# Clustered attention with experts on one core: one tile for the halves of q and k, and placing as ten single steps

## Chip, core and metric

The kernel runs on one NeuronCore of one Trainium2 chip. The metric is device microseconds of one execution; the kernel before took 1026.75 us in the median of 3 runs (1024.31 to 1026.94).

## What is computed

Two things in a row: attention within clusters, over 4 batches x 8 heads x 768 positions of 64 values, with 16 centroids per head, and on its output, as 3072 rows of 512, a layer of 8 experts of which each row uses two. Cut to what matters:

```python
q_n, k_n, c_n = (t / (norm(t) + 1e-6) for t in (q, k, centroids))
q_assign = argmax(einsum('bhsd,hcd->bhsc', q_n, c_n), -1)
k_assign = argmax(einsum('bhsd,hcd->bhsc', k_n, c_n), -1)
scores = where(q_assign[..., :, None] == k_assign[..., None, :], scale * q @ k.T, -1e9)
attn = exp(scores - max(scores))
attn = attn / (attn.sum(-1) + 1e-9)
x = (attn @ v), heads put side by side            # 3072 x 512
logits = x @ w_gate
noisy = logits + log1p(exp(x @ w_noise)) * noise
top2, weights = two largest of noisy, softmax of them
out[row] = sum over its two experts of weight * (relu(x @ w1[e]) @ w2[e])
```

## The kernel before

**Tiling.** Attention works on 16 pairs of heads (4 batches x 4 pairs). A pair takes 12 steps: 2 heads s, 6 chunks kc of 128 keys each. There are 192 steps t in one loop; the values of a step are multiplied 4 steps after its scores. The experts follow behind the loop, on the same engines; their code is not touched.

**One pair p**, in the order in which its work is due:

- `load_qk` (L581) brings q and k of both heads into a tile qt by a DMA on SP's queue; `load_v` (L592) brings v of two pairs.
- `a_hi` (L641) on ScalarE (ACT) and `a_lo` (L654) on VectorE (DVE) split float32 q and k into a high half and the rest, in pieces of 384 columns. They go into a tile **hl** of [128, 4, 768], whose four parts are k low, q high, k high and q low. From pair 2 on, ACT first copies a piece of qt into a PSUM bank (L651), writes the high half from there (L652), and DVE writes the low half (L660). Each pair allocates a new tile named hl from a pool with one buffer, so all lie in the same memory; pair 1 has another tile, xt.
- `b_place` (L722) is ten DMAs on SP's queue (the very first on ACT's) that copy parts of hl to the partitions where the score matmuls read them: into A (L427; three buffers, pair p uses p mod 3) and into Bt, called B in the profile. Four of them go from 64 partitions with 2 x 768 columns, two from 32 partitions with 2 x 768, and four from 32 partitions with 768.
- `a_sims` to `a_eq` find each position's cluster, `a_mask` (L708) turns the clusters into mask rows mk, and `b_mask` (L734) copies them into A with four DMAs.
- `b_max` (L741): PE multiplies halves and mask in A into a PSUM bank (m<-A, L748) and DVE takes the row maxima out of it (mm, L750); 24 of them per pair, in pieces of 128 queries x 384 keys. `b_neg` (L752) makes the negated maxima in high and low halves (nm, L758 to L761); `b_negT` (L763) has PE transpose them (L766) and ACT copy them to nt (L768), and a DMA puts nt into Bt.
- `scores` (L772): for each key chunk and each half of the queries PE multiplies A with A (e<-A, L779) and adds Bt with Bt (e<-B, L780), and ACT writes the exponentials (pe, L781) out of that bank. The two banks e0 and e1 take turns, so a score matmul waits until ACT has emptied its bank. `split_p` (L784) makes the low part pl of the exponentials on GpSimd (POOL; DVE for the last pairs), and `values` (L795) multiplies both parts with v.
- `x_hi` and `x_lo` split a pair's output x into halves xh, `x_put` (L888) stores them to DRAM (xs) on SP's queue, and `x_turn` (L895) copies them transposed into xt. `zero_out` (L852) writes zeros to the output on the same queue, a piece at a time.

**What sets the order.** Every helper call is given a time by `attention()`, and a table MOVE shifts it: the key is the helper's name and arguments (or 'all' for every pair past the first few), the value a number of slots, each a third of a step, and a rank within the slot. The text list FIRST holds the calls ahead of the loop. Each engine and each DMA queue does its work in the order in which the calls come. SP issues a DMA only after the ones ahead of it in its program are issued, and each issue may wait for semaphores. A DMA's end is counted on one of eight semaphores (DMAHW0 to DMAHW7), taken in turn.

In the loop a step's scores stand between the first and second third, and the values of the step four back between the second and the last:

```python
slot(0)
if 0 <= t < z:
    self.scores(t // 12, (t % 12) // 6, t % 6)
if 0 <= t - 1 < z:
    self.split_p((t - 1) // 12, ((t - 1) % 12) // 6, (t - 1) % 6)
slot(1)
...
slot(2)
```

Of the kernel before, what the change touches and what calls it, by code (L numbers as in the profile page):

```python
# [10 lines left out]
F32R = mybir.dt.float32r  # L11
# [86 lines left out]
    ('b_max', 'all', 1, 2, 0): (-1, -3),  # L98
    ('b_max', 'all', 1, 2, 1): (-1, 3),
    ('b_max', 'all', 1, 3, 0): (-1, 0),  # L100
    ('b_max', 'all', 1, 3, 1): (2, 3),
    ('b_max', 'all', 1, 4, 0): (-1, 0.5),
# [20 lines left out]
    ('b_max', 2, 0, 0, 1): (-3, 0),  # L123
# [1550 lines left out]
```

## Time and profile before

| | before |
|---|---|
| median of 3 runs | 1026.75 us (1024.31 to 1026.94) |
| the profiled execution, its own time | 1021.25 us |
| its span in the trace | 1019.4 us |
| PE busy | 943.3 us (93%), 7985 instructions |
| PE weight loads | 613.6 us (60%) |
| DVE busy | 653.6 us (64%) |
| ACT busy | 489.2 us (48%) |
| POOL busy | 568.2 us (56%) |
| mean granted clock of PE | 0.975 |

The span is what the trace shows from first to last instruction; the execution's own time holds 1.85 us more. Weight loads run beside matmuls. The granted clock is that of TensorE: 1.00 is 2.4 GHz, 0.50 is 1.2 GHz, and a figure between them is a mean over time at either. Attention's loop fills the span up to about 456 us, the experts the rest.

### The profile page before, as it was taken

What the parts mean: (1) busy time and instruction counts of PE and PEld (TensorE: products, weight loads), DVE (VectorE), ACT (ScalarE), POOL (GpSimd) and SP (SyncE); (2) the same over time, 40 slices, a digit from 0 to 9 for tenths busy, and PEclk for the clock granted to TensorE, in tenths of its full rate; (3) what the DMA queues carried; (4) which work ended last, traced back from release to release, by engine and by line L of the source; (5) the groups of instructions that cost most, each with busy time, mean ns of one, the idle gap of its engine ahead of it and who ended that gap; (6) DMA issues with size and microseconds to landing.
All of it is one profiled execution on the core that took longest, in us unless ns stands there. A gap on an engine that the chain in (4) does not pass through costs nothing. (4 is left out here: it accounts for less than half of the span.)

```text
span 1019.4 us, 21147 instructions
## 1 busy us (share of the span) xinstructions
PE 943.3 (93%) x7985; PEld 613.6 (60%) x7985; DVE 653.6 (64%) x1401; ACT 489.2 (48%) x1080; POOL 568.2 (56%) x640
## 2 busy tenths in 40 slices
PE   4779899998989899899889999999999999999994
PEld 2567788787868787774455545445455454554542
DVE  5768788797869788986636655546554655555420
ACT  2567677776777766477042415315233153241510
POOL 9558698887999899962435225234243252432311
PEclk9989999998989999999989999999999999999997
DMA  7687798988887776154395925929529267292200
GB/s 191 167 197 172 167 233 204 222 201 213 198 203 190 188 166 139 67 98 118 120 215 153 256 86 155 216 74 245 147 84 265 93 167 216 67 256 89 69 32 31
DMA packets 147148, 162.28 MB, mean 159 GB/s; under 512 B 85433, under 2 KB 112441, under 8 KB 147042
## 3 DMA queue, kind: packets, MB, share of 16 engines
q1 hardware_dynamic: 133612, 123.60, 49.3%
q0 software_dynamic: 12864, 36.37, 12.0%
q10 hardware_dynamic: 566, 0.91, 0.5%
q8 instruction: 64, 1.05, 0.5%
q14 instruction: 42, 0.34, 0.1%
HBM read 77.30 MB, written 26.05 MB: 101 GB/s over the span
## 5 line engine op out<-in xcount | busy, mean ns | idle before, releaser
L792 POOL TENSOR_TENSOR pl<-pe 128x768 f16<-128x768 f32 x173 | 251.3, 1468 | 47.3 <-ACT pe L781 38.1
L750 DVE TENSOR_REDUCE mm<-m 128x1 f32<-128x384 f32 x384 | 198.3, 550 | 47.9 <-PE m L748 47.2
L1561 PEld LDWEIGHTS <-w1t 128*128 128x128 f16 x1536 | 149.8, 98 | 118.3 <-DMA xT<-xg 7.8
L781 ACT ACTIVATE pe<-e 128x384 f32<-128x384 f32 x384 | 167.9, 488 | 94.5 <-PE e L780 87.7
L1602 PEld LDWEIGHTS <-hT 128*128 128x128 f16 x1152 | 112.2, 98 | 133.9 <-issue 1.1
L1614 POOL DMA_INDIRECT out<-yo,idx x50 | 60.2, 1204 | 229.9 <-DVE yo L1610 109.4
L1561 PE MATMUL m<-xT,w1t 128*128 128x400 f16 (+4 forms) x768 | 171.8, 335 | 0.0
L779 PE MATMUL e<-A 128*128 128x384 f32 x384 | 143.3, 373 | 16.3 <-ACT pe L781 16.1
L748 PE MATMUL m<-A 128*128 128x384 f32 x384 | 133.1, 396 | 13.6 <-DMA A<-mk 8.9
L780 PE MATMUL e<-B 128*128 128x384 f32 x384 | 133.7, 348 | 2.5 <-issue 2.5
L1602 PE MATMUL m<-w2t,hT 128*128 128x512 f16 x600 | 132.0, 379 | 0.0
L1561 PE MATMUL e<-xT,w1t 128*128 128x400 f16 (+4 forms) x528 | 122.1, 336 | 7.4 <-DMA xT<-xg 7.4
L1437 DVE TENSOR_TENSOR hT<-hr,hT 128x384 f16<-128x384 f32 (+6 forms) x128 | 70.7, 557 | 78.4 <-ACT hT L1436 77.4
L813 PE MATMUL av<-vv,pe 128*128 128x65 f16 x1152 | 100.4, 197 | 0.0
L815 PE MATMUL av<-vv,pe 128*128 128x64 f16 x1152 | 98.8, 195 | 0.0
L1541 POOL DMA_INDIRECT xg<-xs,idx x50 | 52.6, 1051 | 79.3 <-DMA xT<-xg 69.3
L748 PEld LDWEIGHTS m<-A 128*128 128x128 f32 x384 | 73.6, 200 | 35.5 <-DVE mm L750 13.5
L813 PEld LDWEIGHTS <-pe 128*128 128x128 bf16 x1152 | 78.2, 99 | 23.9 <-issue 20.5
L779 PEld LDWEIGHTS e<-A 128*128 128x128 f32 x384 | 75.6, 197 | 22.1 <-ACT pe L781 19.2
L1434 ACT ACTIVATE hr<-e 128x400 f32<-128x400 f32 (+4 forms) x44 | 22.3, 507 | 137.8 <-PE e L1561 137.8
L815 PEld LDWEIGHTS <-pe 128*128 128x128 bf16 x1152 | 80.4, 100 | 0.0
L1602 PE MATMUL e<-w2t,hT 128*128 128x512 f16 x360 | 79.8, 379 | 0.6 <-ACT w2t L1441 0.5
(282 smaller groups left out, 1448.0 us busy)
## 6 DMA issues: line engine op xcount, KB each, us to landing
stg<-in_moe_w SPq DMA_DIRECT2D x64, 512.0 KB, 4.0
qt<-in_qk SPq DMA_DIRECT2D x15, 768.0 KB, 10.4
A<-hl SPq DMA_DIRECT2D x30, 384.0 KB, 3.7
B<-hl SPq DMA_DIRECT2D x29, 384.0 KB, 6.9
vt<-in_v SPq DMA_DIRECT2D x8, 768.0 KB
out<-zt SPq DMA_DIRECT2D x12, 512.0 KB
A<-hl SPq DMA_DIRECT2D x60, 96.0 KB, 6.5
xs<-xh SPq DMA_DIRECT2D x15, 384.0 KB, 3.5
```

What stands on the lines that cost most here:

```text
L748: nc.tensor.matmul(t, A[:, s, 0, j * 128:j * 128 + 128], A[:, s, 1, n * 384:n * 384 + 384], start=True, stop=True)
L750: nc.vector.tensor_reduce(st["mm"][:, self.NJ * s + j, n:n + 1], t, axis=X, op=OP.max, negate=True)
L779: nc.tensor.matmul(t, A[:, s, 1, ks], A[:, s, 0, ns], start=True, stop=False)
L780: nc.tensor.matmul(t, Bt[:, 0, s, ks], Bt[:, 1, s, ns], start=False, stop=True)
L781: nc.scalar.activation(pe[:, n], t, AF.Exp, scale=self.scale)
L792: (nc.vector if last else nc.gpsimd).tensor_tensor(lo, pe, hi, op=OP.subtract)
L813: nc.tensor.matmul(av[:, j, :], ph[:, js], vv[:, hh, kj, 64:129], start=(kc == 0 and j == 0), stop=False, skip_group_check=True)
L815: nc.tensor.matmul(av[:, j, :64], ph[:, js], vv[:, hh, kj, 0:64], start=False, stop=False, skip_group_check=True)
L1437: nc.vector.tensor_tensor(h1, r[:, a:b], h0, op=OP.subtract)
L1561: nc.tensor.matmul(p, self.w1t[:, wi, c, f * 128:f * 128 + 128], self.xT[e][:, c, xi, n0:n1], start=(i == 0), stop=(i == 3 * ND - 1))
L1602: nc.tensor.matmul(p, self.hT[:, hi, f, t * 128:t * 128 + 128], self.w2t[:, wi, f], start=(i == 0), stop=(i == 3 * NF - 1))
L1614: i = nc.gpsimd.indirect_dma_start(out=self.out, out_offset=bass.IndirectOffsetOnAxis(ap=en[:r], axis=0), in_=yo[:r], in_offset=None, boun ...
```

## The change

- **One tile for the halves.** The tile hl is allocated once, for pair 0, and kept as `self.hl`; pair p from 2 on writes its halves into the same tile. Pair 1 keeps its xt.
- **Placing as ten single steps.** `b_place`, two calls per pair that issue six and four DMAs, becomes `p_hi`, `p_lo` and `p_b` (one DMA each per head s) and `p_a` (one for each head and each of q and k), each with its own time and its own entry in MOVE. The DMAs themselves, their sources, targets and sizes stay.
- **New places.** About 150 entries of MOVE are new, gone or changed, and FIRST has another order. No arithmetic changes.

```diff
 MOVE
...
-    ('a_eq', 2): (-2, 0),
+    ('a_eq', 1): (73, 0),
...
-    ('a_hi', 'all', 0, 0): (1, 3),
-    ('a_hi', 'all', 0, 1): (2, -3),
+    ('a_hi', 'all', 0, 0): (2, 3),
+    ('a_hi', 'all', 0, 1): (1, -3),
...
-    ('a_lo', 'all', 0, 0): (1, -0.5),
-    ('a_lo', 'all', 0, 1): (3, 0.5),
+    ('a_lo', 'all', 0, 0): (2, -0.5),
+    ('a_lo', 'all', 0, 1): (2, 0.5),
...
-    ('a_mask', 2): (-3, 0),
+    ('a_mask', 2): (-1, 0),
...
+    ('b_max', 'all', 0, 0, 0): (4, 0),
+    ('b_max', 'all', 0, 0, 1): (2, 0),
...
-    ('b_place', 'all', 0): (0, 0.5),
-    ('b_place', 'all', 1): (6, 0.5),
...
+    ('load_v', 'all', 1): (-3, 0),
+    ('p_a', 'all', 0, 0): (0, 0.5),
+    ('p_a', 'all', 0, 1): (2, 0.5),
+    ('p_a', 'all', 1, 0): (0, 0.5),
+    ('p_a', 'all', 1, 1): (0, 0.5),
...
+    ('p_b', 'all', 0): (5, 0.5),
+    ('p_b', 'all', 1): (7, 0.5),
...
+    ('p_hi', 'all', 0): (0, 0.5),
+    ('p_hi', 'all', 1): (0, 0.5),
...
+    ('p_lo', 'all', 0): (0, 0.5),
+    ('p_lo', 'all', 1): (4, 0.5),
...
-    ('x_hi', 'all', 0): (4, 0),
-    ('x_hi', 'all', 1): (-1, 0),
+    ('x_hi', 'all', 0): (-2, 0),
+    ('x_hi', 'all', 1): (-4, 0),
...
-    ('x_lo', 'all', 0): (6, 0),
-    ('x_lo', 'all', 1): (-4, 0),
+    ('x_lo', 'all', 0): (-6, 0),
+    ('x_lo', 'all', 1): (-7, 0),
...
+    ('x_put', 'all', 1): (-1, 0),
...
-    ('x_turn', 'all'): (-2, 0),
+    ('x_turn', 'all'): (1, 0),
...
 FIRST
...
-b_place 0 1 0 ACT
+p_lo 0 0 ACT
+p_b 0 0 ACT
 b_max 0 0 5
 b_max 0 0 2
-b_place 0 1 1
+p_lo 0 1
+load_v 0 0
+p_b 0 1
 b_max 0 0 4
-load_v 0 0
-b_place 1 0
+p_hi 1 0
+p_a 1 0 1
+p_hi 1 1
+a_turn 1
 b_neg 0 0 1
-a_turn 1
-b_negT 0 0 1
 load_qk 2
...
+p_b 1 0
+b_negT 0 0 1
+p_b 1 1
...
 attention()
-                        at(w + T["place"], self.b_place, p, i)
+                    for s in range(2):
+                        at(w + T["place"], self.p_hi, p, s)
+                        for i in range(2):
+                            at(w + T["place"], self.p_a, p, i, s)
+                    for s in range(2):
+                        at(w + T["place"], self.p_lo, p, s)
+                        at(w + T["place"], self.p_b, p, s)
...
 a_hi()
-            self.st[p]["hl"] = (self.gp.tile([128, 4, self.S], F32R, name="xt", bufs=1) if p == 1 else
-                                self.pre.tile([128, 4, self.S], F32R, name="hl", bufs=1))
+            if p == 0:
+                self.hl = self.pre.tile([128, 4, self.S], F32R, name="hl", bufs=1)
+            self.st[p]["hl"] = self.gp.tile([128, 4, self.S], F32R, name="xt", bufs=1) if p == 1 else self.hl
...
-    def b_place(self, p, part, s=None, by=None):
-        hl, A, Bt = self.st[p]["hl"], self.A[p % 3], self.Bt[p % 3]
-        for s in range(2) if s is None else (s,):
-            r = 64 * s
-            if part == 0:
-                self.dma(A[0:64, s], hl[r:r + 64, 1:3], by)
-                self.dma(A[96:128, s, 0], hl[r:r + 32, 3], by)
-                self.dma(A[96:128, s, 1], hl[r:r + 32, 2], by)
-            else:
-                self.dma(Bt[0:64, :, s], hl[r:r + 64, 0:2], by)
-                self.dma(Bt[64:96, :, s], hl[r + 32:r + 64, 2:4], by)
+    def p_hi(self, p, s, by=None):
+        self.dma(self.A[p % 3][0:64, s], self.st[p]["hl"][64 * s:64 * s + 64, 1:3], by)
+
+    def p_lo(self, p, s, by=None):
+        self.dma(self.Bt[p % 3][0:64, :, s], self.st[p]["hl"][64 * s:64 * s + 64, 0:2], by)
+
+    def p_a(self, p, i, s, by=None):
+        self.dma(self.A[p % 3][96:128, s, i], self.st[p]["hl"][64 * s:64 * s + 32, 3 - i], by)
+
+    def p_b(self, p, s, by=None):
+        self.dma(self.Bt[p % 3][64:96, :, s], self.st[p]["hl"][64 * s + 32:64 * s + 64, 2:4], by)
```

How this moves instructions, at three places. In these rows the line is that of the file the row belongs to (the changed file is 85 or 86 lines longer at these places), and "waits" are the semaphores that the instruction waits for; m_4465 and the like are PSUM tiles.

**ACT, the first high halves of q of pair 10, before:**

```order
L651 ACTIVATE m_4465<-qt 128x384 [waits DMAHW6_49,DVE_49]
L652 ACTIVATE hl<-m_4465 128x384 [waits DMAHW4_49,DMAHW3_49,DMAHW5_49,DMAHW2_49,DMAHW6_49,DMAHW1_49,DMAHW7_49,DMAHW0_49,Activation_49]
L781 ACTIVATE pe<-e_4471 128x384 [waits PE_49,Pool_49]
L781 ACTIVATE pe<-e_4475 128x384 [waits PE_49]
L651 ACTIVATE m_4509<-qt 128x384 [waits DVE_49]
L652 ACTIVATE hl<-m_4509 128x384 [waits Activation_49]
```

and of the change:

```order
L737 ACTIVATE m_4457<-qt 128x384 [waits DMAHW5_49,DVE_49]
L738 ACTIVATE hl<-m_4457 128x384 [waits DMAHW6_49,DMAHW4_49,DMAHW7_49,DMAHW2_49,Activation_49]
L867 ACTIVATE pe<-e_4461 128x384 [waits PE_49,Pool_49]
L867 ACTIVATE pe<-e_4465 128x384 [waits PE_49]
L737 ACTIVATE m_4499<-qt 128x384 [waits DVE_49]
L738 ACTIVATE hl<-m_4499 128x384 [waits Activation_49]
```

The list of the first hl write shrinks from all eight DMA semaphores to four; the place among the exponentials (pe) is the same here.

**DVE at the same place, from a row maximum of pair 8 to its negation, before:**

```order
L750 TENSOR_REDUCE mm<-m_4461 128x1 [waits PE_49]
L660 TENSOR_TENSOR hl<-m_4465,hl 128x384 [waits DMAHW4_49,DMAHW3_49,DMAHW5_49,DMAHW2_49,DMAHW6_49,DMAHW1_49,DMAHW7_49,DMAHW0_49,Activation_49]
L1041 TENSOR_SCALAR aux<-aux 128x12 [waits DVE_49]
L750 TENSOR_REDUCE mm<-m_4481 128x1 [waits PE_49]
L750 TENSOR_REDUCE mm<-m_4484 128x1 [waits PE_49]
L758 TENSOR_REDUCE aux<-mm 128x12 [waits DVE_49]
L760 TENSOR_SCALAR nm<-aux 128x12 [waits DVE_49]
L761 SCALAR_TENSOR_TENSOR nm<-aux,nm 128x12 [waits DVE_49]
```

and of the change:

```order
L836 TENSOR_REDUCE mm<-m_4453 128x1 [waits PE_49]
L1127 TENSOR_SCALAR aux<-aux 128x12 [waits DVE_49]
L746 TENSOR_TENSOR hl<-m_4457,hl 128x384 [waits DMAHW5_49,DMAHW7_49,DMAHW0_49,Activation_49]
L836 TENSOR_REDUCE mm<-m_4472 128x1 [waits PE_49]
L836 TENSOR_REDUCE mm<-m_4475 128x1 [waits PE_49]
L844 TENSOR_REDUCE aux<-mm 128x12 [waits DVE_49]
L846 TENSOR_SCALAR nm<-aux 128x12 [waits DVE_49]
L847 SCALAR_TENSOR_TENSOR nm<-aux,nm 128x12 [waits DVE_49]
```

The low half stays ahead of the last two row maxima; its list shrinks to three DMA semaphores.

**SP around the placing of pair 9** (A_111 and B_114 are its tiles, nt is that of pair 7), before:

```order
L720 DMA B_115<-nt 2x12x128
L888 DMA xs<-xh 768x1x256
L895 DMA_TRANSPOSE xt<-xh 128x12x128
L588 DMA qt<-in_qk 128x1536
L720 DMA A_111<-hl 64x1536
L720 DMA A_111<-hl 32x768 x2
L720 DMA A_111<-hl 64x1536
L720 DMA A_111<-hl 32x768 x2
L720 DMA B_114<-hl 64x2x768
L720 DMA B_114<-hl 32x2x768
L720 DMA B_114<-hl 64x2x768
L720 DMA B_114<-hl 32x2x768
```

and of the change:

```order
L974 DMA xs<-xh 768x1x256
L806 DMA B_115<-nt 2x12x128
L673 DMA qt<-in_qk 128x1536
L981 DMA_TRANSPOSE xt<-xh 128x12x128
L806 DMA A_111<-hl 64x1536
L806 DMA A_111<-hl 32x768 x2
L806 DMA A_111<-hl 64x1536
L806 DMA A_111<-hl 32x768
L806 DMA B_114<-hl 64x2x768
L806 DMA A_111<-hl 32x768
L806 DMA B_114<-hl 64x2x768
L806 DMA B_114<-hl 32x2x768 x2
```

The store xs now stands ahead of nt, the load of q and k (qt) ahead of the transposing copy, and the last of the four narrow copies into A between the wide ones into B; behind both come v's load, zeros and the mask's four copies.

**SP ahead of the loop** (A_112 and xt belong to pair 1, the last row is the load of pair 2's q and k), before:

```order
L720 DMA B_114<-hl 32x2x768 [waits DMAHW1_49]
L595 DMA vt<-in_v 128x1536 [waits DMAHW2_49]
L720 DMA A_112<-xt 64x1536 [waits DMAHW3_49]
L720 DMA A_112<-xt 32x768 [waits DMAHW4_49,Pool_49]
L720 DMA A_112<-xt 32x768 [waits DMAHW6_49]
L720 DMA A_112<-xt 64x1536 [waits DMAHW7_49]
L720 DMA A_112<-xt 32x768 [waits DMAHW0_49]
L720 DMA A_112<-xt 32x768 [waits DMAHW1_49]
L588 DMA qt<-in_qk 128x1536 [waits DMAHW2_49,PE_49]
```

and of the change:

```order
L680 DMA vt<-in_v 128x1536 [waits DMAHW1_49]
L806 DMA B_114<-hl 32x2x768 [waits DMAHW2_49]
L806 DMA A_112<-xt 64x1536 [waits DMAHW3_49]
L806 DMA A_112<-xt 32x768 [waits DMAHW4_49,Pool_49]
L806 DMA A_112<-xt 64x1536 [waits DMAHW6_49]
L673 DMA qt<-in_qk 128x1536 [waits DMAHW7_49,PE_49]
```

The load of q and k waits for DMAHW7 and no longer for DMAHW2, the semaphore of the second row of the first block (vt).

## Rows read from the trace of the kernel before

**Rows 1.** Windows, attention's middle and the experts: us, busy (x) of five engines, PEclk, DMA share, GB/s.
```profile
48.00:420.00 372.00, 343.63 (x4453) 292.01 (x4450) 297.70 (x766) 261.44 (x605) 314.82 (x286) 0.95 0.79 189
456.00:1019.00 563.00, 540.48 (x2929) 278.63 (x2927) 293.38 (x507) 185.79 (x391) 188.98 (x268) 0.98 0.53 143
```

**Rows 2.** Waits of PE, 48 to 420 us: total us, times, longest us.
```profile
PE e L779 <- ACT pe L781: 14.9, 6, 4.8
PE m L748 <- DMA A<-mk: 6.5, 5, 3.0
```

**Rows 3.** Timeline of PE: start us, us, instruction, [idle before <-releaser].
```profile
118.16 0.69 PE L779 MATMUL e<-A 128*128 128x384 f32 x1 [3.00 <-ACT pe L781]
...
145.16 0.41 PE L748 MATMUL m<-A 128*128 128x384 f32 x1 [0.77 <-DMA A<-mk]
...
191.61 0.44 PE L779 MATMUL e<-A 128*128 128x384 f32 x1 [0.71 <-ACT pe L781]
...
195.05 0.41 PE L748 MATMUL m<-A 128*128 128x384 f32 x1 [1.34 <-DMA A<-mk]
...
242.69 0.44 PE L779 MATMUL e<-A 128*128 128x384 f32 x1 [2.20 <-ACT pe L781]
...
246.08 0.98 PE L748 MATMUL m<-A 128*128 128x384 f32 x2 [1.06 <-DMA A<-mk]
...
299.70 0.66 PE L748 MATMUL m<-A 128*128 128x384 f32 x1 [2.98 <-DMA A<-mk]
...
349.13 0.44 PE L779 MATMUL e<-A 128*128 128x384 f32 x1 [2.90 <-ACT pe L781]
...
375.02 0.44 PE L779 MATMUL e<-A 128*128 128x384 f32 x1 [1.29 <-ACT pe L781]
```

**Rows 4.** Timeline of ACT, DVE and PE around the half-writes at 242 us.
```profile
241.77 0.49 ACT L652 ACTIVATE hl<-m 128x384 fp32r<-128x384 f32 x1 [2.81 <-DMA B<-hl]
...
242.29 0.56 DVE L660 TENSOR_TENSOR hl<-m,hl 128x384 fp32r<-128x384 f32 x1 [2.87 <-DMA vt<-in_v]
...
242.84 1.01 DVE L750 TENSOR_REDUCE mm<-m 128x1 f32<-128x384 f32 x2
...
244.32 0.17 DVE L761 SCALAR_TENSOR_TENSOR nm<-aux,nm 128x12 fp32r<-128x12 f32 x1
...
244.54 0.48 PE L766 MATMUL m<-ident,nm 128*128 128x128 f32 x1 [0.28 <-DVE nm L761]
```

**Rows 5.** Windows, a stretch of 12 us without a long wait; columns as in rows 1.
```profile
204.00:216.00 12.00, 12.00 (x176) 10.83 (x175) 11.49 (x36) 8.12 (x18) 9.93 (x9) 1.00 0.89 215
```

**Rows 6.** Timeline of DVE and PE: the negation and the transpose in pair 5.
```profile
119.24 0.17 DVE L761 SCALAR_TENSOR_TENSOR nm<-aux,nm 128x12 fp32r<-128x12 f32 x1
...
122.11 0.27 PE L766 MATMUL m<-ident,nm 128*128 128x128 f32 x1
```

**Rows 7.** Timeline of SP's issues and PE in pair 7; a row of the DMA issues.
```profile
219.56 0.69 SPq L720 DMA_DIRECT2D B<-nt  x1
220.36 0.58 SPq L888 DMA_DIRECT2D xs<-xh  x1
...
226.02 0.42 PE L779 MATMUL e<-A 128*128 128x384 f32 x1
...
xs<-xh SPq DMA_DIRECT2D x15, 384.0 KB, 3.5
```

**Rows 8.** Windows, three stretches behind waits; columns as in rows 1.
```profile
118.00:121.40 3.40, 3.24 (x24) 2.94 (x25) 1.93 (x7) 3.12 (x8) 2.39 (x2) 0.50 0.80 162
196.50:199.90 3.40, 3.40 (x32) 2.49 (x30) 3.18 (x10) 2.45 (x7) 1.72 (x2) 0.50 1.10 223
244.30:251.10 6.80, 5.50 (x31) 4.75 (x31) 4.22 (x13) 4.18 (x11) 3.27 (x3) 0.50 0.66 133
```

**Rows 9.** Timeline of ACT's issues and PE at the loop's first steps.
```profile
25.69 1.20 ACTq L720 DMA_DIRECT2D B<-nt  x1
...
32.68 0.66 PE L780 MATMUL e<-B 128*128 128x384 f32 x1 [2.47 <-issue]
```

More of the change, by code (lines that the diff above doesn't have):

```diff
@@ L97 @@
     ('b_max', 'all', 1, 1, 1): (-1, 0),
[L98 to L102, printed above, removed]
+    ('b_max', 'all', 1, 2, 0): (6, -3),
+    ('b_max', 'all', 1, 2, 1): (5, 3),
+    ('b_max', 'all', 1, 3, 0): (-4, 0),
+    ('b_max', 'all', 1, 3, 1): (-2, 0),
+    ('b_max', 'all', 1, 4, 0): (-2, 0.5),
+    ('b_max', 'all', 1, 4, 1): (-1, -0.5),
     ('b_max', 'all', 1, 5, 0): (-1, 0),
@@ L122 @@
     ('b_max', 1, 1, 5, 1): (-1, 0),
[L123 removed]
+    ('b_max', 2, 0, 0, 1): (-2, 0),
     ('b_max', 2, 0, 3, 0): (6, 0),
@@ L166 @@
     ('load_qk', 4): (6, 0),
+    ('load_v', 'all', 1): (-3, 0),
[3 more added lines that the diff above has]
+    ('p_a', 'all', 1, 1): (0, 0.5),
+    ('p_a', 2, 0, 0): (3, 0),
+    ('p_a', 2, 0, 1): (3, 0),
+    ('p_a', 2, 1, 0): (3, 0),
+    ('p_a', 2, 1, 1): (3, 0),
+    ('p_a', 3, 0, 0): (2, 0),
+    ('p_a', 3, 0, 1): (1, 0),
+    ('p_a', 3, 1, 0): (1, 0),
+    ('p_a', 3, 1, 1): (1, 0),
+    ('p_b', 'all', 0): (5, 0.5),
+    ('p_b', 'all', 1): (7, 0.5),
+    ('p_b', 1, 0): (76, 0),
+    ('p_b', 1, 1): (76, 0),
+    ('p_b', 2, 0): (3, 0),
+    ('p_b', 2, 1): (3, 0),
+    ('p_b', 3, 0): (1, 0),
+    ('p_b', 3, 1): (1, 0),
+    ('p_hi', 'all', 0): (0, 0.5),
+    ('p_hi', 'all', 1): (0, 0.5),
+    ('p_hi', 2, 0): (3, 0),
+    ('p_hi', 2, 1): (3, 0),
+    ('p_hi', 3, 0): (1, 0),
+    ('p_hi', 3, 1): (1, 0),
+    ('p_lo', 'all', 0): (0, 0.5),
+    ('p_lo', 'all', 1): (4, 0.5),
+    ('p_lo', 1, 0): (76, 0),
+    ('p_lo', 1, 1): (76, 0),
+    ('p_lo', 2, 0): (3, 0),
+    ('p_lo', 2, 1): (3, 0),
+    ('p_lo', 3, 0): (1, 0),
+    ('p_lo', 3, 1): (-3, 0),
     ('total',): (1, 0),
     ('v_max', 'all', 0, 0): (0, -6),
-    ('v_max', 'all', 0, 1): (-3, -1.0),
-    ('v_max', 'all', 1, 0): (-1, 0.0),
-    ('v_max', 'all', 1, 1): (0, 0.5),
+    ('v_max', 'all', 0, 1): (0, -1.0),
+    ('v_max', 'all', 1, 0): (-3, -3),
+    ('v_max', 'all', 1, 1): (-3, 0.5),
+    ('v_max', 0, 0, 0): (1, 0),
     ('v_max', 0, 1, 0): (1, 0),
     ('v_max', 0, 1, 1): (2, 0),
-    ('v_split', 'all', 0, 0): (-1, 0),
-    ('v_split', 'all', 0, 2): (-3, 0),
+    ('v_split', 'all', 0, 0): (-2, 0),
+    ('v_split', 'all', 0, 1): (-2, 0),
+    ('v_split', 'all', 0, 2): (-4, 0),
+    ('v_split', 'all', 0, 3): (-1, 0),
+    ('v_split', 'all', 1, 0): (-1, 0),
+    ('v_split', 'all', 1, 1): (-1, 0),
     ('v_split', 'all', 1, 2): (6, 0),
-    ('v_split', 'all', 1, 3): (0, -3),
-    ('v_split', 0, 0, 0): (-1, 0),
+    ('v_split', 'all', 1, 3): (-3, -3),
+    ('v_split', 0, 0, 0): (-2, 0),
     ('v_split', 0, 0, 2): (1, 0),
@@ L195 @@
     ('x_lo', 1, 1): (1, 0),
+    ('x_lo', 2, 0): (0, -3),
     ('x_max', 0): (-2, 0),
-    ('x_put', 2, 1): (-6, 0),
-    ('x_turn', 'all'): (-2, 0),
+    ('x_put', 'all', 1): (-1, 0),
+    ('x_put', 2, 1): (-2, 0),
+    ('x_put', 3, 1): (-4, 0),
+    ('x_turn', 'all'): (1, 0),
     ('x_turn', 1): (-4, 0),
-    ('x_turn', 2): (-3, 0),
+    ('x_turn', 2): (-7, 0),
+    ('x_turn', 3): (-4, 0),
+    ('zero_out', 10): (-7, 0),
+    ('zero_out', 11): (-10, 0),
+    ('zero_out', 2): (-1, 0),
+    ('zero_out', 3): (-1, 0),
+    ('zero_out', 4): (-1, 0),
+    ('zero_out', 5): (-1, 0),
+    ('zero_out', 6): (-1, 0),
+    ('zero_out', 7): (-1, 0),
+    ('zero_out', 8): (-3, 0),
+    ('zero_out', 9): (-3, 0),
 }
@@ L211 @@
 a_lo 0 0
-b_place 0 0 0
 fixed_init 0
+p_hi 0 0
+p_a 0 1 0
 a_copy 0
@@ L216 @@
 a_max1 0
+fixed_init 1
 a_ge 0
@@ L220 @@
 a_eq 0
-fixed_init 1
 a_hi 1 0
-b_place 0 0 1
+p_hi 0 1
+p_a 0 0 1
+p_a 0 1 1
+p_a 0 0 0
 a_hi 1 1
+a_mask 0
+a_lo 1 0
 a_lo 0 1
-a_lo 1 0
-a_mask 0
 a_lo 1 1
@@ L251 @@
 a_eq 1
-b_place 1 1""".splitlines()
+p_lo 1 0
+p_lo 1 1
+p_a 1 1 0
+p_a 1 1 1
+p_b 1 0
+b_negT 0 0 1
+p_b 1 1""".splitlines()
 def rap(tensor, offset, dims):
```

55 lines of the change are left out of this document (33 added, 22 removed).

## Prediction

> **What bounds the kernel now.** I read the stretches first, then who TensorE waits for, then single waits in order of time. The change touches only what is issued during attention; in the expert stretch, 563 us long, no instruction of its own changes place [rows 1]. In 48 to 420 us PE is busy 343.63 of 372.00 us, and the other engines less: there is 28.4 us of PE idle time to win, plus what a lower clock costs (mean granted clock 0.95) [rows 1]. Of that idle time 14.9 us are six waits of a first score matmul (e<-A) for ScalarE to empty its PSUM bank with the exponentials (ACT pe), and 6.5 us five waits of a row-maximum matmul (m<-A) for the mask's copies [rows 2]. Nine of these waits decide below; they stand one by one [rows 3]. What holds ACT in the first kind is seen at 241.77: it writes the next pair's halves (hl) after waiting 2.81 us for the placing copies of the pair before [rows 4]. The exponentials queue behind that write, so PE stops. One step of the program, by pairs 5 and 15 of the first kind (118.16 and 375.02), is (375.02 - 118.16) / 120 = 2.14 us, so a slot, a third of it, is 0.71 us.
>
> **The change part by part.** Copies, bytes and arithmetic per pair stay the same; only waits and places change.
>
> *1. Halves kept in one tile.* Before, a new tile each pair: its first write waits for all ten copies (the wait list of the order rows). Now the first write of q's high half waits only for the two high-half and the two k copies (p_hi, p_lo), the last of which is eighth of ten; the two p_b, 192 KB each, follow it. At the 215 GB/s that were moved from 204 to 216 us [rows 5] these two take 0.39 MB / 215 = 1.8 us. The write is also one slot later (0.7 us). So ACT's wait shrinks by up to 2.5 us. It would seem that the five waits of the first kind (3.00, 0.71, 2.20, 2.90, 1.29: 10.1 us) [rows 3] nearly go.
>
> But the order rows of VectorE show what is late next. The first low half (hl<-m,hl on DVE) writes the part that p_b reads, so it still waits for the last copy, and behind it on DVE stand the last two row maxima of another pair and their negation, for which PE's transpose at L766 waits. That chain stands in the timeline [rows 4]: low half 242.29, two maxima from 242.84, negation done 244.32 + 0.17, transpose 244.54, behind an idle time of 0.28 us. With ACT free, PE comes to L766 about 2 us sooner and stops there instead. The last copy lands when it landed; what is saved is only that the low half no longer stands behind the 0.49 us of ACT's write: 0.5 us. Pair 5 is the exception: its negation was done at 119.24 + 0.17 while PE reached L766 only at 122.11 [rows 6], so PE may arrive 2.7 us sooner, and 0.5 more from the earlier low half: 3.2 us, which takes in the half-clock stretch 118.0 to 121.4. Pairs 14 and 15 get 0.5 us each; pairs 8 and 10 run into part 2. **Gain 3.2 + 1.0 us** (from 0.5 each, 2.5 us, to 10.1 us).
>
> Pair 3 waited longest (4.8 us) [rows 2]. Its write waits for one p_b less (0.9 us), but the mask of pair 2 now stands behind it on ACT: I set it at 0.
>
> *2. The first row maxima two slots later.* Masks land when the queue lets them: placing copies, v's load and zeros stand before them. A first m<-A that comes 1.4 us later in the program finds the copies landed, or wastes 1.4 us less. Pair 5's wait was 0.77, pair 7's 1.34, pair 9's 1.06, pair 11's 2.98 [rows 3]; with the 0.5 us of part 1 the two middle ones would be 1.84 and 1.56, so 1.4 comes off each of three: **gain 0.8 + 3 x 1.4 = 5.0 us** (0 to 6.2, the sum of the four). What covers the moved maxima is DVE's room later in the pair, and there is little: 11.49 of 12 us in 204 to 216 [rows 5]. Two maxima of 0.5 us (1.01 for two) [rows 4] moved into such a stretch can cost 1.0 us; three pairs stall like this: 0 to 3.0, **I take 1.6 us of loss**, the middle, since PE is full there as well [rows 5].
>
> *3. The store of x (xs) ahead of the negated maxima (nt) on SP, the load of q and k ahead of the transposing copy.* SP issues in order; it stood still until nt could go at 219.56, and xs took the next 0.58 us [rows 7]. Gone ahead, xs lets the placing copies start 0.6 us sooner, which each remaining wait on a landing feels: the rest of pairs 7 and 9 (0.44 and 0.16), pairs 11, 14 and 15 with 0.6: **2.4 us** (0 to 5 x 1.8 if the bytes of xs, 384 KB, leave the queue sooner too).
>
> *4. Clock.* The granted clock is 0.50, the lower of its two levels (1.2 GHz), in stretches right behind such waits: 118.0, 196.5 and 244.3 [rows 8]; the mean of 0.95 [rows 1] stands for some 0.05 x 372 / 0.5 = 37 us of them in all. The time lost is half of PE's busy time in them. That of 118.0 is in part 1. That of 196.5 followed waits of 0.71 and 1.34 us, which nearly go: 3.40 / 2 = **1.7 us** (0 to 1.7). That of 244.3 stays, since its wait moves to L766.
>
> *5. Start.* The load of pair 2's q and k no longer waits for v's load to land (order rows), and so is issued before the first nt, which ACT issued at 25.69; PE's first e<-B had to wait for it until 32.68 [rows 9]. If nt stands behind these 768 KB it lands 0.79 MB / 215 GB/s = 3.7 us later; if the two queues share the engines, not at all. I take a **loss of 1.2 us**, a third, as nt is one of the smallest copies. The Trainium skill (DMA: Bandwidth & Descriptors, section Queues, rings and completion order) says that each DMA engine takes turns between the queues that have work for it, a packet at a time; by that the loss would be near 0 and the gain 1.2 us larger. The 7 us from issue to 32.68 show that turns can still be long here, and the measurement decides.
>
> The other moves (zeros and v's split a few slots earlier, values of x split earlier) I set at 0: POOL and ACT have idle time in this stretch [rows 1]; without it they would delay the low part of the exponentials on POOL, and PE's values behind it.
>
> **Sum:** 3.2 + 1.0 + 5.0 - 1.6 + 2.4 + 1.7 - 1.2 = 10.5 us off the profiled execution, 1021.25 to 1010.7. That execution lies 5.5 us below the median of the runs (1026.75), which is what will be compared: **1016.3 us**.
>
> **Rivals.**
> - *Nothing measurable.* The moved maxima find no room on DVE, so part 2 comes to 0 after its loss, part 3 finds its transfers queued as before, and the start costs 3.7: 4.2 + 1.7 - 3.7 = 2.2 us, 1024.6. For it: DVE at 11.49 of 12. Against: PE waits visibly for masks. That the change doesn't do what it says, and the wait stays whole, belongs here, but the wait lists show it shortened.
> - *Much faster.* The low half on DVE doesn't hold PE, because the copies land sooner once PE no longer stalls: part 1 gives 9.4 us, part 2 its full 6.2, part 3 2.4, the three half-clock stretches half of 3.24 + 3.40 + 5.50 = 6.1 [rows 8]; less 1.2 for the start: 22.9 us, 1003.9. Against it: L766 comes right on the chain, in one pair after the other [rows 4].
> - *Slower.* In SP's order nt now stands behind xs, and xs behind POOL's low half of x. In pair 7 nt was issued at 219.56 and the first scores came at 226.02 [rows 7], 6.5 us later; to land it needs no more than the 3.5 us that the store, a far larger copy of that queue, takes [rows 7], so 3.0 us are left. If xs is held longer than that, PE stops at the first e<-B of the five odd pairs from 7 on; 2 us more each and a half-clock stretch behind it (1.7) make 18.5 us, less the 10.5: 1034.8. It decides at 3.0 us; below that it costs nothing. For it: a new wait in an in-order queue. Against: x's halves are split earlier as well, and xs left 0.8 us after nt without being held.
>
> **How the numbers follow.** Forecast 0.52 (own range 1010 to 1022, from parts 1 to 5 at their nearer bounds), nothing measurable 0.20, much faster 0.13, slower 0.15. A measurement of this kernel can tell 0.3% (3 us) from no change. Faster: 0.50 of the forecast, 0.13, and 0.02 of the second: 0.65. Same: 0.02 + 0.15 + 0.02 of the slower: 0.19. Slower: 0.03 + 0.13 = 0.16. The range reaches from 1004, which leaves out the better half of much faster, to 1030, which leaves out most of slower.
>
> **What would show it.** Right: PE's waits for ACT pe in 48 to 420 us fall from 14.9 to some 6 us, those at L766 for DVE nm come to 4 us or more, mask waits fall to about 2; fewer half-clock stretches; ACT's waits at hl nearly gone, DVE's at hl still there. Wrong: e<-A waits unchanged (the wait moved nowhere), m<-A waits as long as before or DVE the one it waits for, e<-B waiting for nt, or the first e<-B later than 34 us.

## The result and the profile after

The changed kernel took **1008.59 us** in the median of 4 runs (1007.38 to 1011.03), the kernel before 1025.53 us in 4 (1023.22 to 1026.94): ratio 0.984, 95% interval 0.981 to 0.987, 16.9 us between the medians. The forecast was 1016.3 us, from a gain of 10.5 us. The profiled execution after took 1007.38 us, its span is 1005.5 us: 13.9 us below the profiled execution of before, against which the 10.5 us were summed. The other 3 us of the 16.9 come from where the two profiled executions lie among their runs (4.3 us below the median before, 1.2 after).

The stretches, as windows (columns as in [rows 1]): 

```profile
48.00:420.00 372.00, 347.56 (x4630) 293.04 (x4628) 310.94 (x788) 267.67 (x625) 328.64 (x301) 0.99 0.80 189
...
456.00:1019.00 563.00, 526.65 (x2826) 271.60 (x2823) 283.20 (x477) 174.33 (x365) 184.87 (x264) 0.98 0.53 139
```

The same 372 us now hold 4630 instructions of PE, not 4453 [rows 1], at a granted clock of 0.99, not 0.95. For a fair comparison the same work is needed: from the first exponential of pair 1 to the first transpose behind attention. Its two windows, the kernel before first, and then after:

```profile
69.60:454.39 384.79, 357.90 (x4745) 303.70 (x4744) 314.25 (x784) 270.30 (x622) 329.98 (x308) 0.96 0.74 177
```

```profile
69.40:440.11 370.71, 348.48 (x4745) 294.60 (x4743) 312.72 (x785) 268.47 (x623) 329.93 (x309) 1.00 0.78 185
```

The stretch is 14.1 us shorter (384.79 to 370.71), the whole gain. PE's idle time in it fell from 26.89 to 22.23 us (length less busy): 4.7 us. Its busy time for the same 4745 matmuls fell by 9.4 us. That is the clock, by this account: the half-clock stretches from 94 us on, among them those of [rows 8], are gone, as two windows of the kernel after show, one over the only half-clock stretch left in attention and one behind it:

```profile
63.50:70.30 6.80, 5.69 (x55) 4.93 (x56) 2.80 (x5) 5.52 (x12) 2.93 (x2) 0.50 0.87 233
70.30:497.00 426.70, 399.12 (x5043) 319.87 (x5040) 349.64 (x875) 292.18 (x670) 345.66 (x333) 1.00 0.74 177
```

Whom PE waits for in 48 to 420 us, after; lines L865, L834 and L852 are L779, L748 and L766 of before:

```profile
PE m L834 <- DVE mm L836: 7.2, 12, 1.3
PE m L852 <- DVE nm L847: 4.7, 5, 2.3
PE e L865 <- ACT pe L867: 3.7, 4, 1.8
...
PE m L834 <- DMA A<-mk: 1.2, 2, 0.9
```

Against [rows 2] the first scores' waits for ACT fell from 14.9 to 3.7 us and the mask's from 6.5 to 1.2. Two others grew most: for the transposed maxima (L852, 4.7 us; L766 of before waited 2.1 us for them and 1.7 for the low half) and for DVE to empty a bank of row maxima (7.2 us in 12 waits; 0.3 before). So of the 11.2 us that went at the scores at most 2.6 came back at the transposes. Behind ACT and DVE, the waits at the tile hl in the same window, after (ACT waits 1.3 us more for a copy of the mask, 4.1 in all):

```profile
ACT hl L738 <- DMA B<-hl: 2.8, 2, 2.5
...
DVE hl L746 <- DMA B<-hl: 4.6, 2, 2.3
```

The chain that the forecast named stands in one place in full, at 311 us (timeline of DVE and PE): the low half of pair 13 waits for the last copy, two maxima of pair 11 and their negation follow, and PE's transpose waits 2.32 us, as in [rows 4] but with ACT no longer the one that PE waits for.

```profile
311.15 0.56 DVE L746 TENSOR_TENSOR hl<-m,hl 128x384 fp32r<-128x384 f32 x1 [2.33 <-DMA B<-hl]
...
311.73 1.01 DVE L836 TENSOR_REDUCE mm<-m 128x1 f32<-128x384 f32 x2
...
313.43 0.33 PE L852 MATMUL m<-ident,nm 128*128 128x128 f32 x1 [2.32 <-DVE nm L847]
```

And the start, after, against [rows 9]: pair 0's first e<-B comes 1.5 us later than before.

```profile
34.18 0.66 PE L866 MATMUL e<-B 128*128 128x384 f32 x1 [4.58 <-issue]
```

### The profile page after: what moved, and what is told of

It is laid out like the page before. It is cut to its first block, busy times and chain, and to the rows that moved or that the text cites. A ratio compares the mean times of both kernels' runs of the same rounds, so it can differ in the third digit from the quotient of the medians.

```text
span 1005.5 us, 21131 instructions
## 1 busy us (share of the span) xinstructions
PE 935.5 (93%) x7985; PEld 606.2 (60%) x7985; DVE 651.5 (65%) x1401; ACT 487.4 (48%) x1080; POOL 567.1 (56%) x640
## 5 line engine op out<-in xcount | busy, mean ns | idle before, releaser
L834 PE MATMUL m<-A 128*128 128x384 f32 x384 | 130.6, 394 | 14.3 <-DVE mm L836 9.2
L865 PE MATMUL e<-A 128*128 128x384 f32 x384 | 138.9, 362 | 4.7 <-ACT pe L867 4.6
L866 PE MATMUL e<-B 128*128 128x384 f32 x384 | 131.6, 343 | 4.6 <-issue 4.6
L834 PEld LDWEIGHTS m<-A 128*128 128x128 f32 x384 | 70.9, 196 | 35.9 <-DVE mm L836 17.8
L899 PEld LDWEIGHTS <-pe 128*128 128x128 bf16 x1152 | 76.8, 98 | 24.3 <-issue 20.1
L865 PEld LDWEIGHTS e<-A 128*128 128x128 f32 x384 | 74.5, 194 | 8.6 <-ACT pe L867 6.3
L901 PEld LDWEIGHTS <-pe 128*128 128x128 bf16 x1152 | 78.8, 99 | 0.0
```

Source lines behind the costliest of these rows:

```text
L834: nc.tensor.matmul(t, A[:, s, 0, j * 128:j * 128 + 128], A[:, s, 1, n * 384:n * 384 + 384], start=True, stop=True)
L865: nc.tensor.matmul(t, A[:, s, 1, ks], A[:, s, 0, ns], start=True, stop=False)
L866: nc.tensor.matmul(t, Bt[:, 0, s, ks], Bt[:, 1, s, ns], start=False, stop=True)
L899: nc.tensor.matmul(av[:, j, :], ph[:, js], vv[:, hh, kj, 64:129], start=(kc == 0 and j == 0), stop=False, skip_group_check=True)
L901: nc.tensor.matmul(av[:, j, :64], ph[:, js], vv[:, hh, kj, 0:64], start=False, stop=False, skip_group_check=True)
```

## The experiments

Twelve kernels ran in three series of four, each series on one chip beside the kernel before (median 1029.85, 1023.18 and 1022.97 us there), five rounds each. The changed kernel ran in the first and the third series as a mark. Times from different series are compared by their ratios to the kernel before.

| kernel | series | median us | ratio to before, 95% interval |
|---|---|---|---|
| changed kernel (after_again) | 1 | 1016.94 | 0.9862 (0.9831 to 0.9892) |
| new_tile_each_pair | 1 | 1018.62 | 0.9891 (0.9858 to 0.9923) |
| first_maxima_back | 1 | 1021.76 | 0.9931 (0.9903 to 0.9959) |
| filled_waits | 1 | 1031.96 | 1.0016 (0.9993 to 1.0039) |
| two_tiles_before | 2 | 1021.92 | 0.9988 (0.9963 to 1.0013) |
| two_tiles_after | 2 | 1007.59 | 0.9855 (0.9819 to 0.9890) |
| x_places_back | 2 | 1016.47 | 0.9945 (0.9920 to 0.9971) |
| late_qk2 | 2 | 1007.28 | 0.9861 (0.9826 to 0.9895) |
| changed kernel (after_mark) | 3 | 1009.64 | 0.9875 (0.9848 to 0.9901) |
| moves_on_before | 3 | 1011.49 | 0.9893 (0.9863 to 0.9922) |
| store_behind_nt | 3 | 1016.31 | 0.9947 (0.9926 to 0.9968) |
| two_tiles_late_qk2 | 3 | 1003.08 | 0.9805 (0.9777 to 0.9832) |

### The marks

> The changed kernel once more, as the mark for the others on this chip. Every theory expects 0.984 of the kernel before (about 1008.6 us where before takes 1025.5), half-clock time in attention of one stretch (6.8 us, at 63 us) and first score matmuls waiting 3 to 4 us in all for ScalarE.

> The changed kernel as the mark of this series: 0.984 to 0.986 of the kernel before.

Measured 0.9862 and 0.9875; the intervals overlap with each other and with the first result's 0.984. In the first mark's trace pair 15 alone took 7 us longer than in the traces of before and after; it took 5 to 8 us longer in all kernels of that series and in none of the others, so it is not a matter of an edit. The expectation of one half-clock stretch in attention was missed: there are two more, 3.4 us at 43 us and 6.8 us at 429 us, the latter in pair 15.

### What the kept tile is worth

**A new tile again.** The changed kernel with this edit:

```diff
-            if p == 0:
-                self.hl = self.pre.tile([128, 4, self.S], F32R, name="hl", bufs=1)
-            self.st[p]["hl"] = self.gp.tile([128, 4, self.S], F32R, name="xt", bufs=1) if p == 1 else self.hl
+            self.st[p]["hl"] = (self.gp.tile([128, 4, self.S], F32R, name="xt", bufs=1) if p == 1 else
+                                self.pre.tile([128, 4, self.S], F32R, name="hl", bufs=1))
```

> The changed kernel with a new tile hl for each pair again; all places stay. Theory 1 (the kept tile takes the wait off ScalarE): the first write of a pair's high half waits for all ten copies again, ScalarE's waits at hl rise from 4 us to 10 or more in 48 to 420 us, the e<-A waits of TensorE from 3.7 to 8 or more, and at least two half-clock stretches come back: 5 us or more slower than the changed kernel, 1013.6 or above. Rival (the places do it: the last copy is issued only two issues behind the eighth, and the low half on VectorE waits for it in either version): under 2 us slower, 1010.6 or below, and no half-clock stretch but the one at 63 us.

Measured 1.7 us above the mark, ratio 0.9891 against 0.9862 (3.0 us), with intervals that overlap. ACT's waits at hl rose only from 4.2 us (the mark) to 7.8, PE's waits for ACT from 3.8 to 6.2; of theory 1's numbers none was reached, but one half-clock stretch of 3.4 us at 314 us came back. The waits of PE and ACT in 48 to 420 us, first the mark:

```profile
PE m L852 <- DVE nm L847: 4.9, 5, 2.1
PE e L865 <- ACT pe L867: 3.8, 4, 2.1
...
ACT hl L738 <- DMA B<-hl: 3.1, 2, 2.9
```

and with a new tile each pair (its lines stand one lower):

```profile
PE e L864 <- ACT pe L866: 6.2, 5, 2.7
PE m L851 <- DVE nm L846: 2.9, 6, 1.5
...
ACT hl L737 <- DMA B<-hl: 7.5, 4, 3.4
```

The kept tile takes 2.4 us off the waits for ACT, and the waits at the transposes are 2.0 us longer with it. From the first exponential of pair 1 to that of pair 15 both traces take 350.0 to 350.1 us. But for the one stretch the rival holds: with the new places the tile is worth 1.7 to 3 us between the medians, which can't be told from nothing.

**Two tiles in the kernel before.** By then another theory stood: halves and copies take turns in one tile, and that circle sets the pace. In the trace of before ACT's first write of a pair's halves waits for copies in 7 pairs, 16.1 us in all.

```diff
-                                self.pre.tile([128, 4, self.S], F32R, name="hl", bufs=1))
+                                self.pre.tile([128, 4, self.S], F32R, name="hl", bufs=2))
```

> The kernel before with two buffers for the tile hl, so that a pair's halves are written beside the copies of the pair before; no place moves. Loop theory (in the kernel before, writing the halves, some 7.5 us, and copying them, some 17 us, take turns in one tile, and that circle sets attention's pace): ScalarE's waits at hl fall from 16 us to under 2 in 48 to 420 us, the e<-A waits from 14.9 to under 5, most half-clock stretches behind them go, and the time falls to 0.988 of the kernel before or lower, about as much as the whole change. Rival (the queue's bytes set the pace): the waits turn into waits for the mask's or the halves' copies, 0.995 or above.

Measured 0.9988, no gain that can be told. (Its profiled execution took 1026.78 us, 4.9 us above the median of its runs, so the waits of its trace are rather long.) The wait at hl is gone from ACT's list altogether, and nearly all of PE's for ACT with it (14.9 to 1.6 us). But PE's waits in 48 to 420 us now begin so:

```profile
PE m L748 <- DMA A<-mk: 17.0, 5, 4.7
PE av L819 <- POOL pl L792: 3.6, 5, 1.9
PE m L748 <- DMA B<-nt: 2.7, 1, 2.7
...
PE e L779 <- ACT pe L781: 1.6, 1, 1.6
```

What was taken from the scores (13.3 us) came back at the row maxima, which wait for the mask's copies: 6.5 us [rows 2] became 17.0. The rival's numbers came out, and the circle theory falls. Read so, the two kinds of wait in [rows 3] are one wait: for a queue that delivers its copies, in order, too late. Where PE meets it depends on which instruction asks first.

**Two tiles in the changed kernel.** The same edit there:

> The changed kernel with two buffers for hl instead of the one kept tile. Loop theory: the change has brought the circle down to TensorE's own pace, so only its rest is left: the low half no longer holds the transpose (waits there 4.7 to under 3 us), and the time is 0 to 4 us below the changed kernel's 0.986. Rival (the circle still sets the pace): 6 us or more below, 0.980 or lower.

Measured 0.9855, the same as the changed kernel's 0.984 to 0.9875. The transposes' waits fell to 1.8 us, but that shows in no time that could be told from the mark's. (Below, it does together with another edit.)

### What the first row maxima are worth

```diff
-    ('b_max', 'all', 0, 0, 0): (4, 0),
-    ('b_max', 'all', 0, 0, 1): (2, 0),
```

> The changed kernel without its two new entries for the first row maxima (they go back two slots and more). Theory 1 (the later place lets the mask's copies land): waits of m<-A for the mask's copies rise from 1.2 us to 4 us or more, in the odd pairs from 5 to 11, and one or two half-clock stretches come back: 4 to 8 us slower than the changed kernel. Rival (the earlier store and zeros already let the masks land in time): within 1.5 us of the changed kernel, mask waits under 2 us.

Measured 4.8 us above the mark; by the ratios 0.0069, 7.1 us, and the intervals don't overlap. Its waits of PE in 48 to 420 us (its lines stand two lower than the changed kernel's):

```profile
PE m L850 <- DVE nm L845: 4.0, 3, 2.2
PE e L863 <- ACT pe L865: 3.7, 5, 2.1
PE m L832 <- DMA A<-mk: 3.3, 3, 1.9
...
PE m L832 <- DVE mm L834: 2.7, 5, 0.9
```

The mask's waits are back, if less than expected (3.3 us, 0.8 in the mark), and half-clock stretches of 3.4 us each stand at 118 and 193 us. And DVE is waited for 2.7 us here, 6.7 in the mark: the later maxima do crowd DVE, by some 4 us of waits, and pay all the same. In the trace the loss stands nearly all in one place: the steps of pair 5's scores, into which pair 7's first maxima and the stretch at 193 us fall, take 28.4 us and not 24.9.

### What the store's place is worth

**The places of x as before**: the entries of MOVE for x_hi, x_lo, x_put and x_turn are those of before, the rest as changed. In short:

```diff
-    ('x_hi', 'all', 0): (-2, 0),
+    ('x_hi', 'all', 0): (4, 0),
...
-    ('x_lo', 'all', 0): (-6, 0),
+    ('x_lo', 'all', 0): (6, 0),
...
-    ('x_put', 'all', 1): (-1, 0),
-    ('x_turn', 'all'): (1, 0),
+    ('x_turn', 'all'): (-2, 0),
...
```

> The changed kernel with the halves, store and transposing copy of x at the places of before, so that SP issues the store behind the negated maxima again. Theory of part 3 (each pair's placing copies then start some 0.6 us later and every wait for a landing grows): 2 to 5 us slower than the changed kernel (0.988 to 0.991 of the kernel before). Rival (the copies' queue is full anyway, the order on it is indifferent): within 1 us.

Measured 0.9945; its two neighbours of the same series that hold the changed places are at 0.9855 and 0.9861. So 9 us are lost, more than the 2 to 5 expected. The waits show where: 8.3 us at the transposes (4.7 in the changed kernel), as the low half on DVE waits 11.3 us for the last copies (4.6 there).

```profile
PE m L848 <- DVE nm L843: 8.3, 7, 2.3
...
DVE hl L742 <- DMA B<-hl: 11.3, 7, 2.5
```

**The store alone, one place later.** x's halves stay early; only the store goes behind nt on SP:

```diff
-    ('x_put', 'all', 1): (-1, 0),
+    ('x_put', 'all', 1): (0, 3),
```

> The changed kernel with the store of x issued behind the negated maxima on SP, one place later, and everything else as changed (x's halves are split early, the load of q and k stays ahead of the transposing copy). If the store's place in the queue is what part 3 gains (its 384 KB and 0.6 us of issue leave the queue before SP stands still for nt): 5 us or more slower than the mark, 0.990 or above. If the early splitting of x on ScalarE and GpSimd, away from the halves of q and k, is what counts: within 2 us of the mark.

Measured 6.7 us above the mark, 0.9947 against 0.9875, intervals apart: the store's place alone is nearly all of it. The waits grow at the transposes (3.9 us in the mark, 7.6 here) and at the mask's copies (0.5, 3.6). What the store's place does is to be seen on SP. First the mark, SP's issues around the placing of pair 8:

```profile
180.55 3.08 SPq L806 DMA_DIRECT2D A<-mk  x4
184.07 0.58 SPq L974 DMA_DIRECT2D xs<-xh  x1
189.12 0.68 SPq L806 DMA_DIRECT2D B<-nt  x1
189.86 0.39 SPq L673 DMA_DIRECT2D qt<-in_qk  x1
190.36 1.47 SPq L981 DMA_TRANSPOSE xt<-xh  x1
191.94 4.84 SPq L806 DMA_DIRECT2D A<-hl  x5
```

Then the same with the store behind nt:

```profile
180.68 3.32 SPq L806 DMA_DIRECT2D A<-mk  x4
189.25 0.68 SPq L806 DMA_DIRECT2D B<-nt  x1
190.03 0.58 SPq L974 DMA_DIRECT2D xs<-xh  x1
190.66 0.64 SPq L673 DMA_DIRECT2D qt<-in_qk  x1
191.42 1.85 SPq L981 DMA_TRANSPOSE xt<-xh  x1
193.38 5.93 SPq L806 DMA_DIRECT2D A<-hl  x5
```

Both traces stand level up to nt (189.12 and 189.25). Behind it the first placing copy is issued 1.4 us later. And while SP stands still for nt, the copies that it has issued run out. Three windows of each, from 186 to 190 us and on (the mark first; the last two columns are the DMA engines' share and GB/s):

```profile
186.00:190.00 4.00, 3.91 (x51) 3.10 (x49) 3.25 (x10) 3.93 (x12) 3.75 (x3) 1.00 0.87 216
190.00:212.00 22.00, 21.52 (x299) 18.33 (x299) 21.22 (x60) 14.86 (x35) 17.10 (x15) 1.00 0.92 216
212.00:214.00 2.00, 2.00 (x33) 1.73 (x30) 1.07 (x5) 1.72 (x5) 2.00 (x2) 1.00 0.92 248
```

```profile
186.00:190.00 4.00, 3.64 (x51) 2.96 (x49) 3.38 (x10) 3.94 (x11) 3.75 (x3) 1.00 0.50 146
190.00:212.00 22.00, 21.81 (x296) 18.52 (x297) 19.33 (x55) 13.70 (x32) 17.12 (x15) 1.00 0.95 223
212.00:214.00 2.00, 0.39 (x13) 0.26 (x9) 1.90 (x7) 1.46 (x4) 1.19 (x1) 1.00 0.61 175
```

From 190 to 212 us the DMA engines are nearly full in both (0.92, 0.95). In the 4 us ahead they move 216 GB/s with the store ahead of nt and 146 with it behind: 70 GB/s x 4 us = 0.28 MB of the store's 384 KB that must be moved later, when there is no room. At 212 us PE runs on in the one (2.00 of 2.00 us busy) and stands in the other (0.39), at a transpose behind a low half that waits for its copy:

```profile
211.92 0.56 DVE L746 TENSOR_TENSOR hl<-m,hl 128x384 fp32r<-128x384 f32 x1 [1.83 <-DMA B<-hl]
...
214.21 0.33 PE L852 MATMUL m<-ident,nm 128*128 128x128 f32 x1 [1.82 <-DVE nm L847]
```

In the mark the same low half starts at 209.95 us, without a wait. How much of the 1.97 us is the later issue and how much the bytes, the two traces don't tell.

### What the clock is worth

The kernel before with small matmuls ahead of ten waiting ones, in columns of the av bank that nobody reads; no copy or write moves. In short:

```diff
+    def fill(self, n):
+        for i in range(n):
+            self.nc.tensor.matmul(self.avt[:, 400:512], self.identb, self.ones[:, :112], start=False, stop=False,
+                                  skip_group_check=True)
...
     def scores(self, p, s, kc):
+        self.fill({(2, 1, 2): 54, (5, 1, 2): 12, (7, 1, 2): 40, (11, 1, 2): 52, (12, 1, 2): 22}.get((p, s, kc), 0))
...
+        if (s, j, half) == (0, 0, 0):
+            self.fill({5: 12, 7: 24, 9: 18, 11: 54}.get(p, 0))
...
+        self.fill(30 if (p, s) == (2, 0) else 0)
```

> The kernel before, with TensorE kept busy in its waits: small matmuls into columns of a PSUM bank that nobody reads, ahead of the ten matmuls that wait 0.7 to 3.0 us (pairs 2, 5, 7, 9, 11, 12 and one transpose at 91.7 us), sized at some 85% of each wait; no copy or write is moved. Clock theory (most of the gain is the granted clock, which falls behind such waits): the half-clock stretches at 94, 118, 196, 244, 299 and 350 us go (27.2 of 34.1 us), attention gets 8 us or more shorter though no wait was taken away, 1013 to 1018 us. Rival (the copies set the pace, and a faster TensorE only waits longer): the stretches go but the waits grow by as much, 1022 us or more. If the stretches stay, idle time of TensorE is not what they follow.

Measured 1.0016, no gain. Of the six half-clock stretches of before from 94 to 350 us none is left at its place, and two new ones came. One filled place and the new ones, as windows:

```profile
244.00:252.00 8.00, 8.00 (x126) 6.86 (x122) 5.69 (x19) 6.58 (x17) 6.34 (x5) 1.00 0.59 162
...
217.60:224.40 6.80, 5.01 (x31) 4.40 (x32) 4.53 (x14) 4.88 (x12) 2.94 (x2) 0.50 0.15 41
272.20:279.00 6.80, 6.09 (x49) 5.47 (x49) 4.57 (x11) 5.71 (x15) 5.88 (x8) 0.50 0.15 41
```

The new ones stand at waits in pairs that had no filling (timeline of PE):

```profile
219.39 0.69 PE L788 MATMUL e<-A 128*128 128x384 f32 x1 [3.68 <-ACT pe L790]
...
272.91 0.69 PE L788 MATMUL e<-A 128*128 128x384 f32 x1 [2.74 <-ACT pe L790]
```

In 80 to 420 us, 27.2 us at the lower clock became 13.6, and no time was won, while ACT's waits at hl grew from 16.1 to 24.2 us (48 to 420 us):

```profile
ACT hl L652 <- DMA A<-mk: 13.9, 5, 4.3
ACT hl L652 <- DMA B<-hl: 10.3, 6, 3.7
```

The rival's numbers came out: a TensorE that comes sooner waits longer for the copies. The experiment isn't clean: where a wait had moved to another pair, the filling matmuls themselves cost time. And in the profiled execution (1035.08 us, 3.1 above the median of its runs) the 13.6 us came back ahead of 80 us and behind 420 us, so that all of attention holds as much half-clock time as before, 34 us. It shows that filling these waits won nothing, not what the clock alone is worth.

### What the start is worth

```diff
 b_neg 0 0 1
-load_qk 2
...
 b_negT 0 0 1
+load_qk 2
 p_b 1 1
```

> The changed kernel with the load of pair 2's q and k behind the first negated maxima and their copy in the program. Theory of part 5 (the 768 KB ahead delay the 6 KB copy of nt): TensorE's first wait at e<-B falls from 4.6 us to 2.5 or less and pair 0 starts 1 to 2 us sooner; the time is 0 to 2 us below the changed kernel. Rival (the start is bounded by the copies of pair 1 and the mask behind it): the first wait falls, but the first scores of pair 1 come when they came, 0 +- 0.5 us.

Measured 0.9861, as the changed kernel. The first e<-B waits 3.1 us, not 4.6, and pair 0's first exponential comes at 33.6 us, not at 34.9 as in the first trace after. Pair 1's first exponential comes 1.0 us sooner too (68.4 us, 69.4), as the theory had it and not the rival. By itself this can't be told in the time.

### The two moves alone, and the best version

**Moves on the kernel before.** The x entries of the changed kernel and its two entries for the first maxima, in the kernel before. `b_place`, the tile and FIRST stay.

```diff
+    ('b_max', 'all', 0, 0, 0): (4, 0),
+    ('b_max', 'all', 0, 0, 1): (2, 0),
...
-    ('x_hi', 'all', 0): (4, 0),
+    ('x_hi', 'all', 0): (-2, 0),
...
```

> The kernel before with two groups of new places alone: the halves, store and transposing copy of x where the change has them, and the first two row maxima of a pair 4 and 2 slots later. The tile hl stays new for each pair, placing stays in two calls of six and four copies, the start stays. Theory now (these two groups decide, by 8 and 7 us when taken away, and the tile by 0 to 3): 0.990 or lower, 10 us or more below the kernel before. Rival (the parts work only together, as the placing order and the kept tile let the copies start early): 0.995 or above.

Measured 11.5 us below the kernel before in the same series, where the whole change has 13.3: 0.9893 against 0.9875, intervals that overlap. Two groups of places are the change as far as it can be told. ACT's waits at hl, which nothing in this kernel shortens by itself, are 7.8 us, where the kernel before has 16.1: the copies land sooner.

**Two tiles and the later load**, both edits from above in the changed kernel:

> The changed kernel with two buffers for hl and the load of pair 2's q and k behind the first negated maxima, the two edits that came out no slower. If what each saved in its own trace adds up: 3 us below the mark, 0.982 or lower. If attention is at TensorE's own pace by now: within 2 us of the mark.

Measured 1003.08 us, 0.9805 (0.9777 to 0.9832), 6.6 us below the mark, with intervals apart: a version that beats both kernels. Its trace ends attention some 2.7 us sooner than the mark's (the last exponential begins at 433.0 us here, at 435.7 there), and its profiled execution is 1.8 us shorter (1005.49, 1007.32); the rest of the 6.6 us lies in how far each profiled execution is from its median. The trace of two tiles alone ends attention at 433.0 us as well, and its profiled execution took 1005.54 us: no trace shows what the later load adds. Why the two edits give together what neither gave alone is not settled; the intervals of the single ones (0.982 to 0.989) leave room for 2 to 3 us each.

## Why the prediction was right, and where its terms were not

Direction and outer range were right. But the measured 1008.59 us lies below the forecast's own range (1010 to 1022) and nearer to the faster rival (1003.9) than to the forecast (1016.3), and the mechanism of the term with the largest net gain is not what pays.

- **Part 1, the tile (forecast 4.2 us).** Two steps held. With a new tile each pair ACT waits longer at hl (7.8 us, 4.2 in the mark), and where ACT is free and a copy late, the low half on DVE holds the transpose instead (8.3 us there with x's places of before). That is why the bound of 10.1 us was rightly not taken. What was wrong is the share that the tile was given: with all new places but no kept tile, PE's waits for ACT are already 6.2 us and no longer 14.9, and the tile takes off 2.4 more. In time it is 1.7 to 3 us, which can't be told from nothing. The step that failed is "The last copy lands when it landed": with the store gone ahead it lands sooner (the low half waits 4.5 us for it in the third series' mark, 8.9 with the store behind nt). So the waits at the scores fell by 11.2 us, and those at the transposes rose by at most 2.6 (from 2.1 to 4.7), where the prediction let nearly all of them stop.
- **Part 2, the first maxima (forecast 5.0 - 1.6 = 3.4 us).** Right in sign, and the mechanism is there, but the net is 5 to 7 us. The mask's waits that come back with the old places are 2.5 us (0.8 to 3.3), half of the 5.0; two half-clock stretches come with them (6.8 us, so up to 3.4 us of time). DVE's loss was taken as 1.6 us: of the waits for DVE at a row maximum (0.3 us before, 7.2 after) 4.0 go with the old places. These sides don't add up to the time, and the rest stays open.
- **Part 3, the store (forecast 2.4 us).** This term was mis-sized most: 7 us for the store's place alone (0.9947 against 0.9875). Its bound, "0 to 5 x 1.8 if the bytes of xs, 384 KB, leave the queue sooner too", was written down, and the lower price, 0.6 us of issue, was taken. The bytes do leave sooner. The DMA engines' share stood there only over long stretches (0.79 in [rows 1], 0.89 in [rows 5]), and not as a full stretch behind nt and a half-empty one ahead of it. And the bound counted the 5 pairs with a visible wait, while the store stands behind nt in 9 pairs of that run, and in 10 of the kernel before.
- **Part 4, the clock (forecast 1.7 us).** In the account of the trace it is 9.4 of 14.1 us. As a cause it was not separated: filling PE's waits in the kernel before moved half-clock stretches to other waits and gained nothing. Clock and idle time are best counted as shares of what the moves gained, and not as terms beside them.
- **Part 5, the start (forecast 1.2 us of loss).** The first e<-B came at 34.18 us, 1.5 us later, past the 34 us named as a sign against. The copy of 6 KB issued at 25.75 us landed at 34.09, 8.3 us later; where the load stood behind it, it took 6.9 (before, and late_qk2). The Trainium skill (DMA: Bandwidth & Descriptors, section Queues, rings and completion order) has each DMA engine take turns between the queues, a packet at a time. By that the loss would be near 0, and the trace doesn't agree; what held the copy it doesn't show. The 1.5 us cost nothing that could be told alone (late_qk2).
- **The signs.** Waits for ACT (3.7 us, forecast some 6), for the mask (1.2, about 2), at L852 (4.7, 4 or more), fewer half-clock stretches, ACT's waits at hl nearly gone (4.1 us) and DVE's still there (4.6): all came. They would have come with either account of the cause, so they proved the waits and not the parts. Two of the signs against came as well: DVE is the one that m<-A waits for (7.2 us), and the first e<-B is later than 34 us.
- **The rivals.** The slower one (nt held behind xs) did not come; no e<-B in the loop waits for nt. "DVE has no room" was half true: 7.2 us of waits, outweighed. The faster one came in part: the copies do land sooner and the low half stops PE for long at one place only, and the half-clock stretches are gone. But it gave this to a PE that no longer stalls, and the run with the store behind nt shows that it is the store's place.

That the sum of 10.5 us came near the 13.9 us between the profiled executions is luck in part: part 1 was taken too large, parts 2 and 3 too small.

## What to carry to other kernels

When several waits of an engine hang on copies of one in-order queue, they can be one wait: take it away at one place and it stands at the next, as the 13.3 us taken from the scores came back with 10.5 us at the mask. Look for a stretch where that queue runs empty while it waits for something small, and put a large copy that is ready into it; and let the reader of the last copies ask later. Count a queue's free time stretch by stretch, not by the mean share.
